# The last 16 partitions of one expert's w2, loaded in five transfers instead of with the other 112

## The chip, the cores and the metric

The kernel runs on one core of a Trainium2 chip. The metric is the device time of one execution in microseconds (us); the time before is the median of three runs. Profile times count from the first instruction of one profiled execution ("span").

## The reference

An attention over 8 batches, 8 heads, 576 rows and 64 columns is followed by a mixture of 8 experts with 4 slots each. Heads 0 to 3 see a sliding window of 32 rows, heads 4 to 7 every fourth row of the last 128.

```python
scores = where(mask[h], q @ k.T / 8, -1e9);  attn = softmax(scores);  x = attn @ v   # as (4608, 512)
logits = x @ phi                              # (4608, 32)
slot_input = softmax(logits, axis=0).T @ x    # (32, 512), 4 rows for each expert
for e in range(8):
    h = maximum(slot_input[e] @ w1[e], 0)     # w1[e]: 512 x 1024
    slot_out[e] = h @ w2[e]                   # w2[e]: 1024 x 512
out = softmax(logits, axis=1) @ slot_out      # (4608, 512) float32
```

All inputs are float32 in memory; the kernel converts them to float16 as they are loaded.

## The kernel before

**Stages.** A loop over 32 units (8 batches by 4 pairs of heads) computes the attention: `scores`, `softmax_parts`, `values`, `transposes` and the slot sums of finished batches. After the loop follow, in an order written by hand for PE, DVE and ACT, the last units, then the experts: `expert_in` (L764, hidden layer), `expert_turn` (L778, L783), `expert_out` (L793, into the accumulator `sop`). The last two experts' outputs are formed in two column halves (`SIDES`): the first half needs the second row half of expert 6's w2 for these columns and expert 7's w2 for them. When a half of `sop` is complete it is copied to `so` (L860), multiplied with the token weights (`finish_rows`: L830 matmul, L834 or L836 eviction with scaling), and stored by SP (L846). Six of nine output tiles are stored whole (L852) after that.

**Loads.** All loads but three early ones are issued by POOL (GpSimd), whose instructions stay in the order in which the program gives them. They go into one software queue. The q, k and v of all batches come first (`load_batch`, L189 to L215), into eight buffers ("homes"); a home takes an expert's weights when its batch is done with it. Experts 0 to 3 are loaded in pairs (L272, L279); then, from unit 22, w1 of experts 4 and 5 together and w2 of expert 4 (`load_w2(4)`, L302); from unit 26, w1 of expert 6 (L272) and four memsets of `hTp` on POOL (L695); after the loop, w1 of expert 7 (L272), w2 of expert 5 (L302), then w2 of expert 6 and 7 in parts (L295, L286, L311): expert 6's first row half whole, its second in two column halves, expert 7 in pieces of 6 and 2 chunks of each column half.

On chip, w2 of one expert has 128 partitions with 4096 float16 numbers each: partition p holds rows 8p to 8p + 7 of the matrix, 16 KB of float32 in memory that lie in one run.

**What orders the loads.** Each load of the software queue has one of eight semaphores, taken in turn, so a load is issued only when the load eight places earlier has landed. Where a home is still in use, the load waits for PE or DVE as well.

Of the kernel before, what the change touches and what calls it, by code (L numbers as in the profile page):

```python
# [35 lines left out]
OUT_COLS = [sum(nj for _, nj in OUT_TILES[:i]) for i in range(len(OUT_TILES))]  # L36
NU = 4 * B
NV = 2
SIDES = ((0, DMODEL // 2), (DMODEL // 2, DMODEL))
PIECES = ((0, 6), (6, 8))  # L40
HALF = 4
# [5 lines left out]
def kernel(  # L47
# [10 lines left out]
    nc = tc.nc  # L58
# [13 lines left out]
    for n, (nm, ten, by) in enumerate((("qp", q, nc.sync), ("kp", k, nc.scalar))):  # L72
        first[nm] = stage[0:NP, 768 * n : 768 * n + 768].rearrange("p (g x) -> p g x", g=2)
        by.dma_start(
            out=first[nm],
            in_=ten[0, 0:2].rearrange("h s d -> (h s) d").rearrange("(g p r) d -> p g (r d)", g=2, r=RP),
# [3 lines left out]
    def kept(shape, name, dt=FP16):  # L80
        return keep.tile(shape, dt, name=name, tag=name)
# [3 lines left out]
    for n in (1, 2, 4, 8, 16, 32, 64, 128):  # L85
        m = min(n, QW - n)
        nc.vector.tensor_scalar(
            out=count[:, n : n + m], in0=count[:, 0:m], scalar1=float(n), scalar2=None, op0=ALU.add
# [26 lines left out]
    ends = kept([128, 2, 130], "ends")  # L115
    vp = [kept([128, NKB + 1, 4, D + 1], f"vp{i}") for i in range(NV)]
    vd = [kept([128, 16, D + 1], f"vd{i}") for i in range(2)]
# [6 lines left out]
    nc.vector.memset(Pp[0:1, :, 4, 64:128], 1.0)  # L124
    for i in range(NV):
        nc.vector.memset(vp[i][:, :, :, D : D + 1], 1.0)
# [23 lines left out]
        out=ident, in0=count[:, 0:128], scalar1=part, scalar2=None, op0=ALU.is_equal  # L150
# [87 lines left out]
    def select_v(b):  # L238
        raw, last = raws[b]["vp"], raws[b]["vt"]
        for i in range(2):  # L240
            sel = ps_s.tile([128, 2, 2, 4, D], FP32, name=f"sel{b}_{i}", tag="s")
            for r in range(4):
                for n in range(2):
# [8 lines left out]
                    )  # L252
            nc.scalar.copy(out=vp[b % NV][:, 2 * i : 2 * i + 2, :, 0:D], in_=sel[:, :, 0])
        end = ring.tile([128, 2, 4, D], FP32, name=f"sel{b}_2", tag="ring")
        for r in range(4):
# [7 lines left out]
            )  # L263
        nc.scalar.copy(out=vp[b % NV][:, 4:6, :, 0:D], in_=end)

# [18 lines left out]
    def load_half(e, side):  # L284
        d0, d1 = SIDES[side]
        nc.gpsimd.dma_start(  # L286
            out=w_tiles[e][1][:, HALF:8, d0:d1],
            in_=moe_w2[e].rearrange("(p c) f -> p c f", p=128)[:, HALF:8, d0:d1],
        )

    def load_w2(e):
        w2t = w_tiles[e][1]
        w2_from = moe_w2[e].rearrange("(p c) f -> p c f", p=128)
        if e == E_EXP - 2:
            nc.gpsimd.dma_start(  # L295
                out=w2t[:, 0:HALF].rearrange("p c f -> p (c f)"),
                in_=w2_from[:, 0:HALF].rearrange("p c f -> p (c f)"),
            )
            load_half(e, 0)
            return  # L300
        if e < E_EXP - 2:
            nc.gpsimd.dma_start(  # L302
                out=w2t.rearrange("p c f -> p (c f)"), in_=w2_from.rearrange("p c f -> p (c f)")
            )
            return
        w2t = w_tiles[e][1] = w2t.rearrange("p c f -> p (c f)").rearrange("p (s c f) -> p s c f", s=2, c=8)
        for n, (d0, d1) in enumerate(SIDES):
            if n == 1:
                load_half(e - 1, 1)
            for c0, c1 in PIECES:  # L310
                nc.gpsimd.dma_start(out=w2t[:, n, c0:c1], in_=w2_from[:, c0:c1, d0:d1])  # L311
# [148 lines left out]
    def values(u):  # L460
# [11 lines left out]
        for h in range(2):  # L472
            mms = []
            for blk in range(NKB):
                if plain:
                    mms.append((blk, Pp[:, h, blk, 0:128], vp[b % NV][:, blk, hl + h, :]))
                    if blk > 0:
                        mms.append((blk, Pp[:, h, blk - 1, 128:256], vp[b % NV][:, blk - 1, hl + h, :]))
                elif blk < 4:
# [100 lines left out]
    def front_slots(b, up=None):  # L580
# [3 lines left out]
        for n in range(9):  # L584
            j = n % 4
            d0, d1 = (0, DMODEL) if n == 8 else SIDES[n // 4]
            nc.tensor.matmul(  # L587
# [15 lines left out]
    def last_slots(last, dcs):  # L603
        er, x = Er[(B - 1) % 2], xs[B - 1]
        for dc in dcs:
            to = last[:, N_SLOTS * dc : N_SLOTS * dc + N_SLOTS]
            for blk in range(4):
                for g in range(2):
                    d0, d1 = SIDES[g]
                    nc.tensor.matmul(  # L610
# [54 lines left out]
    for u in range(NU - 2):  # L665
# [23 lines left out]
        if u == 22:  # L689
            load_w1(4, 2)  # L690
            load_w2(4)
# [4 lines left out]

    load_w1(E_EXP - 1)
    load_w2(E_EXP - 3)
    load_w2(E_EXP - 2)
    load_w2(E_EXP - 1)  # L700

# [25 lines left out]
    for c in range(2):  # L727
# [14 lines left out]
        out=siT,  # L742
# [45 lines left out]
    def expert_out(e, side=None, chs=range(8)):  # L788
        d0, d1 = (0, DMODEL) if side is None else SIDES[side]
        w2t = w_tiles[e][1][:, side] if e == E_EXP - 1 else w_tiles[e][1][:, :, d0:d1]  # L790
        for ch in chs:
            j = ch % 4
            nc.tensor.matmul(  # L793
                sop[32 * j : 32 * j + 32, d0:d1],
                hTp[e % 4][:, ch, 28 - 4 * e : 60 - 4 * e],
                w2t[:, ch, :],
                start=(e == 0 and ch < 4),
                stop=(e == E_EXP - 1 and ch >= 4),
                skip_group_check=True,
            )  # L800
# [39 lines left out]
    def finish_half(i, side):  # L840
        d0, d1 = SIDES[side]
        ot = ots[i].rearrange("p j d -> p (j d)").rearrange("p (s j d) -> p s j d", s=2, j=4)[:, side]
        rows = out[512 * i : 512 * i + 512, d0:d1].rearrange("(m j) d -> m j d", j=4)
        for j0, j1 in ((0, 2), (2, 4)) if i == 0 else ((0, 4),):
            finish_rows(i, ot, range(j0, j1), d0, d1)
            nc.sync.dma_start(out=rows[:, j0:j1], in_=ot[:, j0:j1])  # L846
# [52 lines left out]
```

## Time and profile before

| | |
|---|---|
| median of 3 runs | 180.75 us (180.22 to 180.85) |
| profiled execution | 180.76 us |
| its span | 178.5 us |
| mean granted TensorE clock | 0.925 |
| busy: PE, DVE, ACT, POOL | 141.9, 127.6, 117.2, 46.6 us |
| packets of the software load queue | 23712, 30.41 MB |
| packets of q1 (stores, three early loads) | 4784, 10.26 MB |
| loads issued by POOL | 66 |

A core has 16 DMA engines. Every load writes one 4-byte packet on each engine after its data, which raises its semaphore; the load has landed when all 16 have. The trace holds the start, length, size and queue of each packet but not the number of its engine. In the page the span is cut into 40 slices of 4.46 us; a digit is the busy share in tenths, DMA is the mean of the 16 engines, GB/s what they moved, and PEclk the TensorE clock that was granted.

### The profile page before, as it was taken

The numbers are of one execution on the slowest core, as the hardware profiler recorded it, in microseconds if no ns is written. First come the engines' busy times: TensorE is split into PE (matmuls) and PEld (weight loads), VectorE is DVE, ScalarE is ACT, GpSimd is POOL, SyncE is SP. The second block draws the span as 40 slices with busy tenths as digits, with TensorE's granted clock in tenths as the row PEclk, the third lists the DMA queues.
The fourth block names the chain that finished last, engine by engine and source line by source line (L and its number), as shares of the span: only waits on it lengthen the run. The fifth ranks groups of instructions, "written<-read, shape, count | busy, mean of one in ns | idle before, by whom it ended". The sixth has DMA issues, their size and how long they took to land.

```text
span 178.5 us, 5128 instructions
## 1 busy us (share of the span) xinstructions
PE 141.9 (80%) x2137; PEld 96.7 (54%) x2137; DVE 127.6 (72%) x360; ACT 117.2 (66%) x217; POOL 46.6 (26%) x74
## 2 busy tenths in 40 slices
PE   6697889889999898989989989999689963897000
PEld 2365666575776676667577667666484421542000
DVE  7968998979889789789798988858821110699300
ACT  2568579878897897897988889777321300699100
POOL 7766444444443544000020050042111100000000
PEclk9988699999999999999999999999996996699855
DMA  5999999999999999999999999999999999999996
GB/s 157 240 199 203 201 199 204 200 205 203 203 200 205 201 204 201 224 218 209 224 213 215 224 207 220 220 206 226 215 206 224 208 196 195 242 385 424 431 420 270
DMA packets 28726, 41.28 MB, mean 231 GB/s; under 512 B 1440, under 2 KB 26016, under 8 KB 26144
## 3 DMA queue, kind: packets, MB, share of 16 engines
q0 software_dynamic: 23712, 30.41, 97.1%
q1 hardware_dynamic: 4784, 10.26, 15.0%
q10 hardware_dynamic: 208, 0.29, 0.6%
q8 instruction: 16, 0.26, 0.5%
q14 instruction: 6, 0.05, 0.1%
HBM read 61.93 MB, written 9.44 MB: 400 GB/s over the span
## 4 chain that ended last, share of the span: by engine, by line
PE 38%; DMA 19%; ACT 16%; DVE 14%; issue 4%; POOL 3%; DVEq 0%; ACTq 0%; POOLq 0%
DMA home<-in_moe_w_dram 14%; PE o L486 9%; PE rgx L506 6%; ACT qT L343 5%; PE l L524 5%; DMA home<-in_q_dram 5%; ACT pr L407 4%; PE sel L256 4%; DVE x L491 4%; ACT ot L834 4%; DVE P L433 3%; PE s L381 3%; PE sel L245 3%; PE f L830 3%; PE u L587 2%
## 5 line engine op out<-in xcount | busy, mean ns | idle before, releaser
L491 DVE TENSOR_TENSOR x<-o,rc 128x640 f16<-128x640 f32 x32 | 26.3, 822 | 0.4
L414 ACT ACTIVATE pd<-s 128x640 f16<-128x640 f32 x32 | 21.9, 713 | 2.2 <-PE s L390 2.2
L407 ACT ACTIVATE pr<-s 128x960 f16<-128x960 f32 (+1 forms) x32 | 22.8, 764 | 0.0
L836 DVE TENSOR_SCALAR ot<-f,rrow 128x256 f32<-128x256 f32 (+1 forms) x24 | 13.0, 612 | 6.9 <-PE f L830 6.9
L486 PE MATMUL o<-vd,P 128*128 128x65 f16 x256 | 14.6, 198 | 3.6 <-DVE x L491 3.0
L486 PEld LDWEIGHTS <-P 128*128 128x128 f16 x288 | 12.3, 100 | 7.5 <-DVE x L491 4.1
L512 ACT COPY xT<-rgx 128x512 f16<-128x512 f16 x16 | 9.4, 589 | 10.6 <-PE rgx L506 10.6
L423 DVE TENSOR_TENSOR Pp<-pr,fixed 128x1280 f16<-128x1280 f16 (+1 forms) x32 | 15.6, 501 | 0.1
L486 PE MATMUL o<-vp,Pp 128*128 128x65 f16 x288 | 15.4, 197 | 0.0
L506 PE MATMUL rgx<-fixed,x 128*128 128x128 f16 x155 | 14.0, 222 | 1.7 <-ACT qT L358 0.8
L272 POOL DMA_DIRECT2D home<-in_moe_w_dram x5 | 3.2, 635 | 45.6 <-PE rgq L353 44.1
L343 ACT COPY qT<-rgq 128x576 f16<-128x576 f16 x16 | 10.2, 639 | 6.8 <-PE rgq L342 6.1
L215 POOL DMA_DIRECT2D home<-in_q_dram x15 | 10.0, 668 | 16.2 <-DMA home<-in_v_dram 11.8
L433 DVE TENSOR_TENSOR P<-pd,fixed 128x1024 f16<-128x1024 f16 x16 | 10.9, 679 | 4.7 <-ACT pd L414 4.7
L189 POOL DMA_DIRECT2D home<-in_v_dram x17 | 11.9, 702 | 8.5 <-DMA home<-in_k_dram 4.0
L486 PEld LDWEIGHTS <-Pp 128*128 128x128 f16 x288 | 11.9, 100 | 3.8 <-issue 2.1
L506 PEld LDWEIGHTS <-x 128*128 128x128 f16 x160 | 10.2, 98 | 6.7 <-issue 4.4
L834 ACT ACTIVATE ot<-f,rrow 128x256 f32<-128x256 f32 (+1 forms) x24 | 12.2, 600 | 2.2 <-PE f L830 1.4
L358 DVE COPY kTd<-rgk 128x576 f16<-128x576 f16 x16 | 12.4, 775 | 1.3 <-PE rgk L353 1.3
L830 PE MATMUL f<-so,ET 128*128 128x256 f16 (+1 forms) x48 | 11.4, 361 | 2.2 <-ACT ot L834 1.0
L343 ACT COPY kTp<-rgk 128x576 f16<-128x576 f16 x16 | 10.3, 644 | 2.0 <-PE rgk L342 2.0
L358 ACT COPY qT<-rgq 128x576 f16<-128x576 f16 x16 | 10.3, 641 | 2.0 <-PE rgq L353 1.4
(133 smaller groups left out, 319.0 us busy)
## 6 DMA issues: line engine op xcount, KB each, us to landing
home<-in_moe_w_dram POOLq DMA_DIRECT2D x5, 2048.0 KB, 35.5
home<-in_q_dram POOLq DMA_DIRECT2D x15, 288.0 KB, 10.2
home<-in_k_dram POOLq DMA_DIRECT2D x15, 288.0 KB, 11.0
home<-in_moe_w_dram POOLq DMA_DIRECT2D x4, 1024.0 KB, 28.0
out_dram<-ot SPq DMA_DIRECT2D x4, 1024.0 KB, 9.4
home<-in_v_dram POOLq DMA_DIRECT2D x6, 512.0 KB, 12.7
out_dram<-ot SPq DMA_DIRECT2D x4, 512.0 KB, 3.8
out_dram<-ot SPq DMA_DIRECT2D x1, 2048.0 KB, 7.7
```

Source lines behind the costliest of these rows:

```text
L343: nc.scalar.copy(out=dst[:, 0:S].rearrange("c (p r) -> c p r", r=RP), in_=rg.rearrange("c r p -> c p r"),)
L358: (nc.scalar.copy if nm == "q" else nc.vector.tensor_copy)(out=dst[:, 0:S].rearrange("c (g p a) -> c g p a", g=4, a=3), in_=rg.rearrange(" ...
L407: nc.scalar.activation(out=(pr[:, :, 0 : 3 * QW], pr[:, :, 3 * QW :])[part], in_=st[:, :, 0 : (480, 224)[part]], func=AF.Exp, scale=SCALE,)
L414: nc.scalar.activation(out=pr[:, part].rearrange("p c e t -> p e c t"), in_=st[:, :, 0 : 2 * DW].rearrange("p e (c t) -> p e c t", c=2), f ...
L423: nc.vector.tensor_tensor(out=Pp[:, :, b0 : b0 + nb, 0:w], in0=pr[:, :, b0 * QW : b0 * QW + nb * w].rearrange("p h (t c) -> p h t c", c=w) ...
L433: nc.vector.tensor_tensor(out=P1.rearrange("p a c t -> p (a c) t"), in0=pr[:, :, :, 0:128].rearrange("p a c t -> p (a c) t"), in1=mask[:, ...
L486: nc.tensor.matmul(ot[:, h, blk], lhs, rhs, start=(n == 0), stop=(n == len(mms) - 1), skip_group_check=True)
L491: nc.vector.tensor_tensor(out=xs[b][:, :, 2 * D * hp : 2 * D * hp + 2 * D].rearrange("p t (h d) -> p h t d", h=2), in0=ot[:, :, :, 0:D], i ...
L506: nc.tensor.transpose(rg[:, 128 * blk : 128 * blk + 128], x[:, blk, hl : hl + 128], ident)
L830: nc.tensor.matmul(fp, ET[:, c0 : c0 + 127 * nj + 1 : nj], so[:, d0:d1], start=True, stop=True)
L834: nc.scalar.activation(out=ot[:, j], in_=fp, func=AF.Copy, scale=scale)
L836: nc.vector.tensor_scalar(out=ot[:, j], in0=fp, scalar1=scale, scalar2=None, op0=ALU.mult)
```

## The change

w2 of expert 4 is no longer loaded by one transfer of 128 partitions. The first 112 partitions are loaded by one transfer with two dimensions on chip. The last 16 come in five, for which a row is seen as two halves of 2048 columns: columns 1984 to 2047 of both halves of partitions 112 to 114; columns 0 to 1983 of both halves of partitions 112 to 119; columns 1984 to 2047 for 120 to 127; columns 0 to 1983 for 120 to 127; columns 1984 to 2047 for 115 to 119. Each of the five has three dimensions on chip (partition, half, column). The bytes moved are the same. w2 of expert 5, the other expert of this branch, is loaded as before, and POOL issues 71 loads instead of 66.

```diff
+LEVEL = (4,)
...
         if e < E_EXP - 2:
-            nc.gpsimd.dma_start(
-                out=w2t.rearrange("p c f -> p (c f)"), in_=w2_from.rearrange("p c f -> p (c f)")
-            )
+            whole = w2t.rearrange("p c f -> p (c f)"), w2_from.rearrange("p c f -> p (c f)")
+            if e not in LEVEL:
+                nc.gpsimd.dma_start(out=whole[0], in_=whole[1])
+                return
+            nc.gpsimd.dma_start(out=whole[0][0:112], in_=whole[1][0:112])
+            halves = [ap.rearrange("p (a x) -> p a x", a=2) for ap in whole]
+            for p0, p1, x0, x1 in (
+                (112, 115, 1984, 2048), (112, 120, 0, 1984), (120, 128, 1984, 2048),
+                (120, 128, 0, 1984), (115, 120, 1984, 2048),
+            ):
+                nc.gpsimd.dma_start(out=halves[0][p0:p1, :, x0:x1], in_=halves[1][p0:p1, :, x0:x1])
             return
```

## The prediction

> **What bounds the kernel now.** I read the page's slices and queues first, then the chain that ended last, then the timeline near the last weight loads, the issues on POOL, and last the single packets of the trace. From the page:
>
> ```profile
> PEclk9988699999999999999999999999996996699855
> DMA  5999999999999999999999999999999999999996
> GB/s 157 240 199 203 201 199 204 200 205 203 203 200 205 201 204 201 224 218 209 224 213 215 224 207 220 220 206 226 215 206 224 208 196 195 242 385 424 431 420 270
> ...
> q0 software_dynamic: 23712, 30.41, 97.1%
> q1 hardware_dynamic: 4784, 10.26, 15.0%
> ...
> q8 instruction: 16, 0.26, 0.5%
> ```
>
> The DMA row is 9 from the second slice to the last but one: the transfers are the bound throughout, loads up to about 154 us and stores after it. The 16 packets of q8, 16 KB each (0.26 MB), are fetches of instructions that run on the same engines. The chain agrees:
>
> ```profile
> 125.28 25.41 DMA home<-in_moe_w_dram
> 150.69 0.04 issue
> 150.73 0.41 PE sop L793 x2
> 151.15 0.02 issue
> 151.17 0.38 ACT so L860
> 151.55 0.04 issue
> 151.59 2.72 PE f L830 x12
> ```
>
> A weight load sets the time up to 150.7. Then the first column half of the output begins: L793, L860, L830, the evictions, the store. The timeline:
>
> ```profile
> 149.99 1.14 PE L793 MATMUL sop<-home,hTp 128*32 128x256 f16 x8 [1.71 <-DMA home<-in_moe_w_dram]
> ...
> 152.79 5.60 SPq L846 DMA_DIRECT2D out_dram<-ot  x7
> ```
>
> PE idles 1.71 us for that load; the first store is issued at 152.79 and its first packet starts at 153.71. From there the stores follow each other without a gap (256 KB every 0.68 us, 1024 KB every 2.45). So the end moves one for one with the landing of that load, the 128x2x256 piece of expert 7's first side (call it I), on the slowest of the 16 DMA engines.
>
> The packets say which engines are slow. A weight row of 8192 bytes on chip takes one packet, and successive rows on one engine start 606 ns apart, so the packets sort into 16 chains, one for each engine, though unnamed; I could follow 14 of them to I. Eight land I at 147.4 to 149.1 us (six of them by 147.9); the other six at 150.1, 150.2, 150.3, 150.4, 150.5 and 150.7. Up to three microseconds separate engines that move the same bytes. The cause shows in the chains: whenever a 16 KB fetch record appears (one about every 8 us, 26.8 to 154.8 on the trace's clock, which is 10.56 ahead of the span's), one chain falls back by some 1.1 us and stays back. By my reading of the chains eight engines take all of these fetches, two each, and eight take none. DMA is full, so nobody catches up.
>
> **The change part by part.** Rows: 112 partitions are 7 rows on each engine in place of 8, 606 ns less for all. The last 16 rows return in pieces of 3, 8, 8, 8 and 5 partitions: two large ones (8 partitions x 2 x 1984 elements) with all but 64 columns of each half-row, three small ones with those 64 columns. No traced transfer has fewer than 16 equal shares, so where they go is not shown. Dealt in turn, one partition to the next engine, they make 32 = 2 x 16 shares; the second and the fourth piece start 16 shares apart, so both large pieces fall on the same eight engines, and the small ones on the other eight twice. This is the arithmetic that I take, since it is the only reading by which three small pieces have this order.
>
> Loaded engines: two rows in 4 packets of 3968 bytes. The 4096-byte packets of L295 follow each other after 305 ns, so 295 each: 4 x 0.295 - 0.606 = +0.57. Relieved engines: -0.606, and 4 packets of 128 bytes. The trace has none; the nearest are phi's 256-byte packets, 22 ns apart (41 long), and 512-byte ones 41 apart. I take 22: +0.09, at most 0.16. All engines: every traced load ends with one 4-byte packet per engine, 21 ns; five more loads make +0.11. Sum: **relieved -0.41 (to -0.34), loaded +0.68 us**.
>
> If the relieved eight are those that take the fetches, the slowest land I at 150.7 - 0.4 = 150.3, and the fast eight at 148.1 to 149.8 stay ahead: the end moves by -0.4. If the last engine is a loaded one, the end moves by up to +0.68.
>
> The Trainium skill ("DMA: Bandwidth & Descriptors", section on why a DMA increments its semaphore by 16) says that a software-generated transfer that cannot use all 16 goes to consecutive engines from a round-robin cursor; by that rule the five pieces fall as dealt above, and no row here says where the cursor stands. Its rules for kernel authors speak against the change: transfers below 64 KB are mostly overhead.
>
> POOL: five more issues at about 0.54 each (L302's 536 ns), 2.7 us, beside this:
>
> ```profile
> 103.77 0.55 POOL L272 DMA_DIRECT2D home<-in_moe_w_dram  x1 [13.29 <-PE rgq L353]
> 104.31 1.83 POOL L695 MEMSET hTp<- 128x480 f16 x4
> 118.45 0.53 POOL L272 DMA_DIRECT2D home<-in_moe_w_dram  x1 [12.31 <-PE rgq L353]
> ...
> 139.58 0.70 POOL L311 DMA_DIRECT2D home<-in_moe_w_dram  x1 [4.04 <-DMA home<-in_moe_w_dram]
> ```
>
> POOL idles 13.3 us there, so the issues cost nothing. But each load waits for the load eight earlier (the eight semaphores of the software queue are taken in turn), and five more loads move everything behind them by five places. The fourth piece waits for experts 0 and 1's w2 (95.1 on its slowest engine), the fifth for the next pair's w1 (about 105), w1 of expert 6 for their w2 (114.6, issued at 103.8 before), then the memsets of hTp. Those are read from about 139. w1 of expert 7 waits for experts 4 and 5's w1: 124.4 instead of 118.5. w2 of expert 5 follows when the 112 rows have landed, about 129; the next five as the pieces land, 129 to 133; the last two as before, about 134 and 139. The fastest engine reaches w1 of 7 at 131.2 at the earliest and w2 of 5 at 136.1, so the queue stays fed by 6 us. Zero, and one microsecond for each that a load comes later than that.
>
> PE, ACT, DVE: the same instructions with other semaphores; expert 4's matmuls (142.5) wait for pieces that landed about 13 us before. Zero. SP's stores are unchanged.
>
> The profiled execution took 180.76 (span 178.5 and 2.3 around it) against a median of 180.75, so 180.76 - 0.41 = 180.35.
>
> **The rivals.**
> *Wrong eight.* The last of the fetch-taking engines is a loaded one: +0.68 if it is the one at 150.7, +0.1 to +0.5 if it is one of the other five; 180.9 to 181.45. For it: engines are unnamed and nothing in the profile ties the dealing to them; a shift of the deal by a few turns a gain into this loss. Against: the odd 3 in front and 5 behind make sense only to shift the eight. It decides as soon as one engine now beyond about 149.7 is loaded. This is the side on which the kernel gets slower.
> *No levelling.* The pieces are spread over all 16, or the software puts one partition on each engine: only semaphores and smaller packets, +0.1 to +0.25, so 180.85 to 181.0. Against: 3 and 5 do not divide over 16.
> *A starved queue.* The later issues leave the engines empty before w1 of 7 or w2 of 5. It decides where a wait lasts 6 us longer than above; 1 to 3 us, 181.8 to 183.8.
> *A fixed price for each transfer.* If each extra load held the queue for a time that its bytes do not explain, five would add up. The nearest row is the 64 KB tail of v (L189, 16x8x256): eight packets and its semaphore hold an engine 8 x 0.041 + 0.021 = 0.35 us, with no gap to the next load. With that as the price of each, +1.75, so 182.5. The Trainium skill (same page, anatomy of one DMA) puts a fixed 2 us on each; five in a row would be an estimate of 10 us by that page, which the gapless tail speaks against.
>
> **How the numbers follow.** Levelling as summed 0.50 (180.1 to 180.5); wrong eight 0.27; no levelling 0.08; starved or fixed price 0.08; something that also takes an idle stretch away, under 179.85, 0.07. What a measurement can tell from no change is about 0.5%, 0.9 us, so both large cases lie mostly inside it. Faster 0.10: the last case and the lower tail of the first. Slower 0.18: starved or fixed price, and a wrong eight in which the small pieces cost more than 22 ns a packet. Same 0.72. The range reaches from the first case with some scatter (three runs lie 0.6 us apart) to the wrong eight with dearer packets: 179.9 to 181.7. The likeliest case alone: 180.0 to 180.6.
>
> **What would show it.** Right: the wait of L793 for the 128x2x256 load and the first store's issue (152.79) come 0.4 us earlier, the spread of I's landings falls from 3.3 us to about 2.2, w2 of expert 4 takes 7 rows and four half-rows on eight chains, and the stores keep their spacing. Wrong: I lands later on its slowest chain while the spread grows to 4.4 us (wrong eight), all chains shift alike (no levelling), or a hole in the DMA share between 126 and 140 us (starved queue). A longer time with unchanged I would mean that the stores, not this load, set the end.

## The result, and the profile after

The change made the kernel slower by a little: 180.95 us (median of 14 runs, 180.78 to 181.12) against 180.38 (14 runs of before), a ratio of 1.0025 with a 95% interval of 1.0015 to 1.0035, +0.45 us by the ratio and +0.57 by the medians. The forecast was -0.41. The profiled execution after took 180.94, with a span of 179.1. That of before, 180.76, lies near the top of the runs of before (180.11 to 180.86), so below the size of an effect is taken from ratios, and the two traces only say where it sits.

The slices and queues of the page after:

```profile
DMA  5999999999999999999999999999999999999995
GB/s 153 239 200 202 201 199 206 200 205 201 205 201 204 200 205 200 224 216 221 212 214 220 214 221 210 216 221 210 209 223 210 210 197 189 260 377 428 428 423 243
...
q0 software_dynamic: 23936, 30.41, 96.9%
q1 hardware_dynamic: 4784, 10.26, 14.9%
...
q8 instruction: 16, 0.26, 0.5%
```

DMA is as full as before: no hole between 126 and 140 us. q0 has 224 more packets for the same bytes. The timeline around the last wait, which answers to 149.99, 150.73 and 152.79 of before:

```profile
150.57 0.40 PE L802 MATMUL sop<-home,hTp 128*32 128x256 f16 x6 [1.49 <-DMA home<-in_moe_w_dram]
...
151.25 0.29 PE L802 MATMUL sop<-home,hTp 128*32 128x256 f16 x2 [0.28 <-DMA home<-in_moe_w_dram]
...
151.58 0.37 ACT L869 CAST so<-sop 128x256 f16<-128x256 f32 x1 [6.31 <-PE sop L802]
...
152.99 5.16 SPq L855 DMA_DIRECT2D out_dram<-ot  x6
```

PE is released at 151.25 in place of 150.73, half a microsecond later instead of 0.4 earlier. The load after it is late by as much. The chain of waits of before has, where the second half of `so` is copied,

```profile
155.19 0.44 DVE so L860
```

and after:

```profile
140.15 15.08 DMA home<-in_moe_w_dram
155.22 0.04 issue
155.26 0.41 PE sop L802 x2
155.68 0.03 issue
...
155.77 0.43 DVE so L869
```

Here the last load of all (the second column half) releases the last matmuls. Its last packet ends at 154.94 (before 154.38, +0.56), the last store at 177.82 (177.27, +0.55); on any one engine that load lands 4.0 us after I, so both move together. The step "the end moves with the slowest engine's landing" holds; the sign of the move was wrong.

POOL after:

```profile
91.47 1.69 POOL L313 DMA_DIRECT2D home<-in_moe_w_dram  x3
95.95 0.55 POOL L313 DMA_DIRECT2D home<-in_moe_w_dram  x1 [2.79 <-DMA home<-in_moe_w_dram]
105.64 0.57 POOL L313 DMA_DIRECT2D home<-in_moe_w_dram  x1 [9.14 <-DMA home<-in_moe_w_dram]
115.66 0.59 POOL L273 DMA_DIRECT2D home<-in_moe_w_dram  x1 [9.45 <-PE rgk L351]
...
125.41 0.56 POOL L273 DMA_DIRECT2D home<-in_moe_w_dram  x1 [7.34 <-PE o L495]
129.81 0.53 POOL L305 DMA_DIRECT2D home<-in_moe_w_dram  x1 [3.84 <-DMA home<-in_moe_w_dram]
```

The fourth and fifth piece, w1 of 6, w1 of 7 and w2 of 5 are issued 0.6 to 1.1 us after the times of the forecast (95.1, about 105, 114.6, 124.4, about 129), which are landings. For w1 of 6 and of 7 the page names PE as the releaser. The loads eight places earlier close last at 114.75 and 124.46, and the issue follows 0.9 us later in both. Where the page names the DMA the distance is much the same (the 112 rows close last at 128.72, w2 of 5 is issued at 129.81). So these two waits are likely for the landing as well.

**Where the pieces fell.** Right behind the 112 rows each chain carries the packets of its pieces: 3968-byte ones 295 ns apart, 128-byte ones 12 ns apart, and two 4-byte packets for each of these six loads, with or without a share. Three patterns occur, on 8, 5 and 3 chains: both large pieces; the small pieces of 8 and 5 partitions; those of 3 and 8. That is the deal of the prediction, partition by partition in turn. Call the engine that gets row 0 of a full load turn 0. Then the large pieces are on turns 3 to 10, the small ones on 11 to 15 and 0 to 2. The landing of the 112 rows, in us, shows how late each of these engines was before any piece moved (in the tables and for single chains, a landing is the start of the first closing packet, which takes 0.02 us):

```
turns 3-10  (large pieces)   125.84 126.15 126.24 127.43 127.44 127.85 127.99 128.37
turns 11-15 (small, 8 and 5) 125.98 128.46 128.52 128.63 128.72
turns 0-2   (small, 3 and 8) 126.18 126.56 126.84
```

Nine engines are 1.5 us or more behind the first; five of them got a double load and four were relieved. The chain that ends last is a loaded one: 112 rows at 127.44, w1 of expert 6 landed at 133.58, then 1.12 us lost at the fetch of 136.02, I at 150.90 (before, the last chain has it at 150.34), last load at 154.91. The first chain has I at 147.19 (before 147.38), so the spread of its landings grew from 2.96 to 3.71 us, the sign that the prediction gave for the wrong eight.

### The profile page after: what moved, and what is told of

The parts are those of the page before. It is cut to its first block, busy times and chain, and to the rows that moved or that the text cites. A ratio compares the mean times of both kernels' runs of the same rounds, so it can differ in the third digit from the quotient of the medians.

```text
span 179.1 us, 5138 instructions
## 1 busy us (share of the span) xinstructions
PE 144.3 (81%) x2137; PEld 97.4 (54%) x2137; DVE 127.3 (71%) x360; ACT 117.0 (65%) x217; POOL 49.4 (28%) x79
## 4 chain that ended last, share of the span: by engine, by line
PE 38%; DMA 19%; DVE 16%; ACT 13%; issue 6%; POOL 0%; DVEq 0%; ACTq 0%; POOLq 0%
DMA home<-in_moe_w_dram 19%; PE o L495 8%; ACT qT L352 5%; PE rgx L515 5%; ACT pr L416 4%; PE sel L257 4%; PE l L533 4%; PE sel L246 3%; DVE x L500 3%; DVE ot L845 3%; PE warm L467 3%; PE s L390 2%; DVE P L442 2%; PE f L839 2%; PE u L596 2%
## 5 line engine op out<-in xcount | busy, mean ns | idle before, releaser
L352 ACT COPY qT<-rgq 128x576 f16<-128x576 f16 x16 | 10.2, 638 | 7.3 <-PE rgq L351 6.6
L273 POOL DMA_DIRECT2D home<-in_moe_w_dram x5 | 3.3, 658 | 37.5 <-PE rgq L362 19.3
L246 PE MATMUL sel<-home,pick 32*128 32x256 f16 x128 | 10.5, 289 | 1.3 <-ACT pr L416 1.3
L216 POOL DMA_DIRECT2D home<-in_k_dram x15 | 9.8, 653 | 6.3 <-DMA home<-in_q_dram 2.9
```

The costliest lines, as they stand in the source:

```text
L216: nc.gpsimd.dma_start(out=parts[nm], in_=src)
L246: nc.tensor.matmul(sel[:, n, 0], pick[rows, r].rearrange("p i j -> p (i j)"), raw[rows, :, r, :], start=(r == 0), stop=(r == 3), tile_posi ...
L352: nc.scalar.copy(out=dst[:, 0:S].rearrange("c (p r) -> c p r", r=RP), in_=rg.rearrange("c r p -> c p r"),)
```

## The experiments

Three theories. **A**: the time depends on which engines get the large shares; first form, the eight that take the fetches stand side by side in the deal, on turns 7 to 14. **B**: the extra transfers themselves cost. **C**: any unevenness costs whoever carries it, so no choice of engines gives a gain. Medians of before, measured beside each group of these runs, were 180.29 to 180.34 us. In each diff the lines replace the list of pieces (first partition, end, first column, end).

**Even.** Five loads more, as in the change, but each over all 16 partitions:

```diff
-(112, 115, 1984, 2048), (112, 120, 0, 1984), (120, 128, 1984, 2048), (120, 128, 0, 1984), (115, 120, 1984, 2048)
+(112, 128, 0, 1792), (112, 128, 1792, 1856), (112, 128, 1856, 1920), (112, 128, 1920, 1984), (112, 128, 1984, 2048)
```

> 112 partitions as in the change, then five pieces of all 16 remaining partitions (columns 0 to 1791 and four times 64 of both halves), so every engine gets the same share: five more loads, the same order and waits on POOL, no levelling. Theory A: all chains move alike by the extra packets, +0.1 to +0.3 us, and the spread of the landings stays as before. Theory B: +0.5 to +0.6 us, as in the change itself.

Measured 180.52, ratio 1.0002 (0.9992 to 1.0012). B falls: the loads, the small packets, their semaphores and the shift of POOL's waits cost nothing that can be measured.

**Turn 0.** Four pieces, the large ones on turns 0 to 7:

```diff
+(112, 120, 0, 1984), (112, 120, 1984, 2048), (120, 128, 0, 1984), (120, 128, 1984, 2048)
```

> Four pieces: large, small, large, small, eight partitions each; the large ones fall on turns 0 to 7. Theory A: seven loaded chains are fast and one (turn 7) is slow, so the end depends on that one chain: +0.1 to +0.6 us, by how late turn 7 was before. Theory B: four extra loads in place of five, so +0.4 to +0.5 us.

Measured 180.77, ratio 1.0018 (1.0006 to 1.0029), about +0.3 us. That lies in A's wide range and, by its interval, in B's as well, so this run decides nothing.

**Turn 15 and turn 7.** A first piece of 7 partitions and then either a small or a large one: the large ones on turns 15 and 0 to 6, or on 7 to 14.

```diff
 turn15
+(112, 119, 1920, 1984), (112, 120, 1984, 2048), (112, 120, 0, 1920),
+(120, 128, 1984, 2048), (120, 128, 0, 1920), (119, 128, 1920, 1984)
 turn7
+(112, 119, 1920, 1984), (112, 120, 0, 1920), (112, 120, 1984, 2048),
+(120, 128, 0, 1920), (120, 128, 1984, 2048), (119, 128, 1920, 1984)
```

> Six pieces in place of five, ordered so that the two large ones start 15 turns after the deal's start (turns 15 and 0 to 6) and the small ones fall on turns 7 to 14 and, once, on the rest. Theory A (the deal is right, and the eight engines that take the instruction fetches are turns 7 to 14, since in the changed kernel's packets four loaded and four relieved chains are slow, and the slow relieved ones show the packet order of turns 11 to 14): all eight loaded chains are fast ones, the slowest landing of the 128x2x256 load comes 0.3 to 0.4 us earlier than before, and the time is 0.2 to 0.4 us under the kernel before (ratio 0.998 to 0.999). Theory B (extra transfers cost time wherever they fall): six extra loads in place of five, so 0.6 to 0.7 us over before (1.003 to 1.004).

> The same six pieces as in the kernel with turn 15, with one small piece moved by one place, so that the large ones start at turn 7 (turns 7 to 14). Theory A: all eight loaded chains are slow ones; the slowest landing of the 128x2x256 load moves by +0.6 to +0.7 us against before, and so does the time (1.003 to 1.004). Theory B: the same time as with turn 15.

Measured 181.0, 1.0029 (1.0017 to 1.0041), and 181.49, 1.0056 (1.0042 to 1.007). The order of the two is as A has it, but turn 15 brings no gain. Both have six pieces, and that is one too many for POOL, here in turn 7:

```profile
115.16 0.56 POOL L317 DMA_DIRECT2D home<-in_moe_w_dram  x1 [9.16 <-DMA home<-in_moe_w_dram]
125.34 0.59 POOL L273 DMA_DIRECT2D home<-in_moe_w_dram  x1 [9.62 <-PE o L499]
125.92 1.83 POOL L708 MEMSET hTp<- 128x480 f16 x4
129.59 0.56 POOL L273 DMA_DIRECT2D home<-in_moe_w_dram  x1 [1.84 <-DVE x L504]
```

With one load more in front, the load eight places before w1 of 6 (L273, 125.34) is w1 of 4 and 5, which closes last at 124.38, and no longer experts 2 and 3's w2 as in the change (115.66). The page again names PE; the landing 1 us earlier is the likelier cause. The pieces queued before w1 of 6 are small. The rows of stretches (last columns: clock, DMA share, GB/s) of turn 7, then of the change, show the engines running dry:

```profile
126.00:129.00 3.00, 2.05 (x32) 1.30 (x32) 2.37 (x7) 1.07 (x3) 1.75 (x4) 1.00 1.03 183
...
132.00:136.00 4.00, 3.45 (x46) 3.33 (x44) 1.06 (x4) 0.90 (x4) 2.77 (x4) 0.93 1.01 182
```

```profile
126.00:129.00 3.00, 2.02 (x32) 1.30 (x32) 2.37 (x7) 1.34 (x3) 0.00 (x0) 1.00 1.08 212
...
132.00:136.00 4.00, 3.44 (x51) 3.14 (x51) 1.13 (x4) 0.53 (x4) 2.75 (x4) 0.92 1.02 213
```

183 and 182 GB/s against 212 and 213. Added up over the 16 engines, the packets of turn 7 leave them empty for 6.8 us between 125.8 and 130 and for 10 us between 131 and 136.5; those of the change for 0.3 us and not at all. This is the starved queue of the prediction, one load beyond the change.

**Ahead 12 and ahead 4.** The five pieces of the change unaltered; the deal is shifted by a transfer of some 128-byte shares into an unused tile, long before, and shifted back after the last load:

```diff
+    deal(12, 0)    # 12 partitions x 2 x 64 columns, after the last q, k and v loads; ahead4: deal(4, ...)
...
+    deal(4, 68)    # after the last weight load; ahead4: deal(12, ...)
```

> The change as it is, with the deal moved on by 12 turns by one more small load (12 partitions x 2 x 64, into a spare tile that nothing reads) before the first weights, and by 4 more after the last load, so that one execution still moves it by a multiple of 16. The five pieces, their sizes and the place of the waits stay. Theory A (turns 7 to 14 take the fetches; the two kernels with six pieces were slow because w1 of expert 6 and of 7 were then issued too late: holes in the DMA work near 127, 133 and 147 us): all loaded chains are fast ones, no holes, the slowest landing of the 128x2x256 load 0.3 to 0.4 us earlier than before, the time 0.2 to 0.4 us under the kernel before (0.998 to 0.999). Theory B (splitting off these pieces costs about 0.6 us wherever they fall): 0.5 to 0.8 us over before, as in the change.

> The same with 4 turns ahead of the pieces and 12 after the last load: the large pieces fall on turns 7 to 14. Theory A: all loaded chains are those that take the fetches, no holes, +0.6 to +0.8 us against before (1.003 to 1.005), a little over the change. Theory B: the same as with 12 ahead.

Measured 180.72, 1.0017 (1.0004 to 1.0029), and 181.25, 1.0043 (1.0029 to 1.0057). PE's last wait, ahead 12 and then ahead 4:

```profile
151.03 0.29 PE L812 MATMUL sop<-home,hTp 128*32 128x256 f16 x2 [0.26 <-DMA home<-in_moe_w_dram]
```

```profile
150.69 1.06 PE L812 MATMUL sop<-home,hTp 128*32 128x256 f16 x8 [1.76 <-DMA home<-in_moe_w_dram]
```

In ahead 4 the eight matmuls stand in one row, and the last of them starts late in its 1.06 us: `so` is copied at 151.79 against 151.35 in ahead 12. The same transfers cost 0.5 us more or less by where they fall, so A's main claim holds. Turn 15 and turn 7 cost 0.2 us more than their twins here, which the dry stretches would explain; the intervals overlap, so that price is not shown. But relieving turns 7 to 14 (ahead 12) still costs 0.3 us, so the first form of A falls. The landings of the 112 rows in ahead 12 say why:

```
turns 15, 0-6 (large pieces) 125.85 126.02 126.35 126.37 127.01 127.51 128.04 128.29
turns 7-11                   126.10 126.18 127.33 127.46 128.57
turns 12-14                  128.47 128.54 128.66
```

Two loaded engines are slow ones. The later of them (128.29) lands I at 150.63 and the last load at 154.65, last of all. Second form of A: slow are 11 to 14, two of 4 to 6, two of 7 to 10.

**Few 15 and few 11.** Now the large shares go to five turns, three for each, and the one left over to the next turn. Five pieces, the small ones filling the rest of each round; 15 or 11 empty shares ahead:

```diff
+(122, 128, 64, 2048), (112, 122, 1984, 2048), (112, 117, 0, 1984), (117, 128, 0, 64), (117, 122, 64, 1984)
...
+    deal(15, 0)    # few11: deal(11, 0)
...
+    deal(12, 68)   # few11: deal(16, 68)
```

> Counting turns of the deal from the kernel before (turn 0 gets row 0 of each full load). The 16 rows go in five pieces of 6, 10, 5, 11, 5 partitions, dealt from turn 15 (15 empty shares of 128 bytes ahead, 12 after the last load): the three large ones all begin at turn 15, so turns 15 and 0 to 3 get six packets of 3968 bytes (for the last rows, two of 3840), turn 4 two, and turns 5 to 14 none, only 128-byte ones. By the measured packets: 6 x 0.295 - 0.606 + 0.11 = +1.28 us on five engines, about +0.1 on turn 4, -0.28 to -0.47 on ten. Theory A, revised: turns 15 and 0 to 3 take no instruction fetches, the eight that do are 11 to 14, two of 4 to 6 and two of 7 to 10. Then no loaded engine is a slow one; the fast ones land I near 149.2 at the latest, and the end moves by -0.3 to -0.45 if turn 4 is without fetches (ratio 0.9975 to 0.9985) and by about +0.1 (1.000 to 1.001) if turn 4 takes them. Theory C: unevenness of the deal costs whoever carries it (another resource binds, or the fetches follow the load): the five with triple load end last and the time rises by 0.7 us or more (1.004 or above).

> The same five pieces with 11 empty shares ahead in place of 15 (16 after the last load in place of 12): the triple load falls on turns 11 to 15, turn 0 gets one large share, turns 1 to 10 are relieved. Theory A, revised: turns 11 to 14 are slow engines, so I lands last about 1.28 us later than before, 1.0060 to 1.0075 (about 1.3 us); against few15 the same bytes in the same transfers differ by 1.2 to 1.7 us. Theory C: as few15, the two within 0.3 us of each other.

Measured 180.5, 1.0016 (1.0003 to 1.0029), and 181.73, 1.0079 (1.0067 to 1.0091). Few 15 and few 11:

```profile
150.77 0.40 PE L812 MATMUL sop<-home,hTp 128*32 128x256 f16 x2 [0.26 <-DMA home<-in_moe_w_dram]
```

```profile
151.18 1.03 PE L812 MATMUL sop<-home,hTp 128*32 128x256 f16 x8 [1.58 <-DMA home<-in_moe_w_dram]
...
152.67 1.65 PE L849 MATMUL f<-so,ET 128*128 128x256 f16 x7 [0.46 <-ACT so L879]
```

The two differ by 1.1 us with the same transfers, which C does not allow, but few 15 gives neither number of A. Its packets: turn 4 is a fast engine (125.80), the ten relieved land I by 149.89, and yet one chain is at 150.39. That is one of the five with triple load, whose 112 rows landed at 127.48, 1.4 us after the earliest of the five. An engine can be late without taking the 16 KB fetches. The trace does not show all of the loss: the profiled execution (180.47) is one of the faster ones, PE's last wait ends at 150.77 against 150.73 in the first kernel, and four of the twelve runs took 180.87 to 181.24. What those four lost is in no trace.

**Few 754 and few 844.** The rounds get 7, 5 and 4, then 8, 4 and 4 partitions, so that turn 3 has two large shares and then one:

```diff
 few754
+(121, 128, 64, 2048), (112, 121, 1984, 2048), (112, 117, 0, 1984), (117, 128, 0, 64), (117, 121, 64, 1984)
 few844
+(120, 128, 64, 2048), (112, 120, 1984, 2048), (112, 116, 0, 1984), (116, 128, 0, 64), (116, 120, 64, 1984)
...
+    deal(15, 0)
...
+    deal(13, 68)
```

In the two texts that follow, "at C" is the landing of w1 of expert 6.

> In the profile of few15 the last chain at C (134.19) and at I (150.39) is one of the five with triple load: its 112 rows landed 1.3 us behind the fastest (127.48); the ten without large share are done with I by 149.86 and turn 4 by about 149.9, where the kernel before has 150.34. The runs of after, ahead4 and ahead12 point to turn 3 as that chain. Here the three large pieces have 7, 5 and 4 partitions, all dealt from turn 15: turns 15, 0, 1, 2 carry three large shares, turn 3 two, turns 4 and 5 one each, turns 6 to 14 none. Theory A: turn 3 lands I at 150.39 - 0.59 = 149.8; the end is set by the relieved slow ones and turn 4 at about 149.9: -0.45 us, ratio 0.9970 to 0.9982, a version faster than both kernels, if turn 5 is not a slow engine; if it is, about +0.5 on it, 150.3 and a ratio of 1.000. Theory C (unevenness costs as such; the late chain was late because it was loaded three times, whichever it is): turns 15 to 2 are still triple, 1.0010 to 1.0020 as in few15.

> few754's packets show turn 3 (the only chain with two large shares) to be 1.8 us behind the fastest at the 112 rows (127.73) and last at C (133.86) and at I (150.07). Here the three large pieces have 8, 4 and 4 partitions, all dealt from turn 15: turns 15, 0, 1, 2 carry three large shares, turns 3 to 6 one each, turns 7 to 14 none. Theory A: turn 3 lands I 0.6 us earlier, about 149.5; the chains with triple load land near 149.2, turns 4 to 6 near 149.9 and the relieved at or below 149.9; the end moves by -0.4 to -0.5 us against the kernel before, ratio 0.9972 to 0.9985, and by -0.1 to -0.25 against few754. Theory C (a deal cannot give more than it takes; few754 is a tie by chance): 0.999 to 1.001.

Measured 180.23, 0.9993 (0.9983 to 1.0002), and 180.19, 0.9989 (0.9979 to 1.0000). Few 754, then few 844:

```profile
150.45 0.40 PE L812 MATMUL sop<-home,hTp 128*32 128x256 f16 x2 [0.26 <-DMA home<-in_moe_w_dram]
...
152.51 0.91 SPq L865 DMA_DIRECT2D out_dram<-ot  x2
```

```profile
150.49 0.29 PE L812 MATMUL sop<-home,hTp 128*32 128x256 f16 x2 [0.27 <-DMA home<-in_moe_w_dram]
...
152.43 2.65 SPq L865 DMA_DIRECT2D out_dram<-ot  x4
```

PE's last wait ends 0.3 us before that of few 15 and 0.24 to 0.28 before that of the first kernel. In few 754 the only chain with two large shares is turn 3's: 112 rows at 127.73, w1 of 6 at 133.86 and I at 150.07, both last. In few 844 it has 127.66 and is no longer last. Its four kinds of chain separate the engines best:

```
turns 15, 0-2 (three large shares) 126.12 126.37 126.47 127.10
turns 3-6     (one)                125.88 127.66 128.15 128.31
turns 7-14    (none)               126.05 126.12 127.31 127.43 128.30 128.41 128.55 128.63
```

With turn 4 fast and turn 3 at 127.66, turns 5 and 6 are slow, and few 754 came out near what A has for a slow turn 5 (1.000). The last chain now is one of these, with its one large share: w1 of 6 at 133.88, I at 150.09. So the gain of 0.4 to 0.5 did not come: about 0.2 us are left, with an interval that reaches to no change and into C's range (0.999 to 1.001). That no deal gains is thus not excluded by the time. Few 844 is faster than the changed kernel (0.9989 against 1.0025); that it beats the first one is likely and not settled.

## Why the prediction was wrong

**The step that failed** is "if the relieved eight are those that take the fetches", taken at 0.50 since "the odd 3 in front and 5 behind make sense only to shift the eight". That was an inference from the shape of the edit, not from a row. The runs show the eight takers to be turns 5, 6, 11, 12, 13, 14 and two of 7 to 10. All tables above fit this, and in the change, ahead 12 and few 844 so does a count: by the landing of the 112 rows 14 fetches were due, six of the takers are late by some two of them and two by one. The two late by one stand on turns 7 to 10 there, and the two fetches still to come last 948 or 949 and 945 ns. In few 11 the two still to come last 974 ns each, and the two chains late by one are among turns 11 to 15 (127.27 and 127.43). That fits a fetch of a given length going to the same engine in each of these traces. Four of the eight stand among turns 3 to 10. No window of eight turns relieves all of them, so an even split into a loaded and a relieved eight cannot reach the gain; the first form of A made the same mistake, that takers stand side by side. The rival "wrong eight" (0.27; 180.9 to 181.45) is what happened, at its lower end.

**The sizes held.** From w1 of 4 and 5 to w1 of 6, a chain of before takes 9.73 us; after, loaded chains take 10.40 (+0.66, forecast +0.68), relieved ones 9.27 (-0.47, forecast -0.41 to -0.34). The 128-byte packets are 12 ns apart, below the 22 that were taken, and the six loads of the change write two 4-byte packets each per engine, where one was taken (in even the same number of loads writes one each). The prediction's 150.7 for the slowest I was 0.4 too late: the last chain has 150.34, and PE goes on 0.39 us after it (after 0.35, few 754 0.38, few 844 0.40). That moved nothing, since only differences were used.

**The deal held.** One partition goes to the next engine, both large pieces to the same eight. The Trainium skill ("DMA: Bandwidth & Descriptors", section "Why a DMA increments its semaphore by 16 and not by 1") has a software transfer that divides over fewer than 16 engines go to consecutive ones from a cursor, and all 16 post the semaphore. The traces agree: 8, 5 and 3 chains by pattern, and the semaphore packets on all 16.

**No levelling, starved queue, fixed price.** None happened in the change. Even (1.0012 at the top of its interval) bounds a fixed price for five loads at 0.2 us. The Trainium skill ("DMA: Bandwidth & Descriptors", section "Anatomy of one DMA — SWDGE (gpsimd) path") gives a fixed 2 us per DMA; behind the full queue of this kernel they do not add up. The starved queue came with one load more (turn 7), where w1 of 6 is issued 9.7 us later than in the change. The difference between turn 7 and ahead 4 puts it at about 0.2 us, not at the 1 to 3 us of that rival.

**Stores and engines** kept their spacing (2.45 us for 1024 KB) and their order, as said.

**Late without the 16 KB fetches.** Turn 3 is late by 1.4 to 2.0 us, and one more engine, turn 1 or 2 (in the change among 0 to 2, in few 11 among 1 to 10), by about 0.7 to 1. Each trace has six 8 KB fetches of q14, a second queue of instructions (322 ns long), between 17 and 118 us. In few 754, where turn 3 alone has two large shares, the fetch of 118.06 ends at 118.38, and the row that starts there is on turn 3's chain (112 rows at 127.73). The row that starts at the end of the fetch of 98.58 is on the other late chain (126.82). The same two chains fit in the change, ahead 12, ahead 4, few 15 and few 844. The fetch near 116 set its engine back by 0.5 us, the one near 97 by 0.3. So the eight that take no 16 KB fetch were not alike either, which the prediction did not see.

**Left open.** Which two of turns 7 to 10 take the 16 KB fetches, and whether the four earlier fetches of q14 make up the rest of the lag; they were not followed.

## What to carry to other kernels

Where the DMA engines are full to the end, the slowest engine sets the time, and work that lands on engines unevenly (instruction fetches here) decides which engine that is. Before bytes are moved from one engine to another, find out which engines are late: put a recognisable pattern of small packets on each turn, as the pieces did here, and read each chain's landing; do not infer it from the shape of the split. A split that loads four engines three times (few 844, 0.9989) beat one that loads eight twice (ahead 12, 1.0017), because the loaded must all be early, and eight early neighbours did not exist.

## What the runs showed of the hardware

- The 16 KB instruction fetches (16 in each execution) go round eight of the 16 engines, which are not neighbours in the deal. Their lengths repeat, within a few ns and but for one or two in a trace, in a cycle of eight (949, 945, 936, 975, 974, 961, 893, 892 ns) that starts at another place from trace to trace, and one set its engine back by 1.1 us. The Trainium skill ("Runtime: NRT & Kernel Launch", section "Instruction fetch mechanics") calls the cost of crossing such a 16 KB boundary mostly hidden. For the engine that runs the program that may be so; here it is paid by the loads, about 2 us on eight of the DMA engines.
- The 8 KB fetches of q14 near 97 and 116 us fell on two further engines, turn 1 or 2 and turn 3, and set them back by 0.3 and 0.5 us.
- In a full queue a 128-byte packet costs its engine 12 ns, and a whole load without a share on that engine about the same (its two closing packets).
- Late engines stay late: in before a chain that lands expert 4's w2 1.02 us after the first (127.33 and 126.31) lands I 1.02 us after it (148.40 and 147.38).
